# Packed attention into a two-product MoE layer: a first phase laid out as one written plan for five queues, with the first attention in parts of the array

## The chip, the cores and the metric

One core of a Trainium2 chip. The metric is the device time of one execution in microseconds (us), as a median of several runs. The profile is a separate execution, taken by the hardware profiler.

## The reference

Eight batches of eight heads, 576 rows of 64 numbers in each head. 32 packed queries `p` attend to `k` and `v`, the rows `q` attend to the result, and the outcome goes through two matrix products with a gate between them. The weights come as 64-bit floats, all else as 32-bit floats.

```python
def sm_attn(qq, kk, vv):                     # scale = 1/8
    s = scale * np.matmul(qq, kk.transpose(0, 1, 3, 2))
    a = np.exp(s - np.max(s, axis=-1, keepdims=True))
    a = a / (np.sum(a, axis=-1, keepdims=True) + 1e-09)
    return np.matmul(a, vv)
p_packed = sm_attn(p, k, v)                  # 8 x 8 x 32 x 64
x = sm_attn(q, p_packed, p_packed)           # 8 x 8 x 576 x 64, heads side by side: 4608 x 512
h = x @ w_in                                 # 512 x 2048
out = (h * np.clip(h + 3.0, 0.0, 6.0) / 6.0) @ w_out
```

## The kernel before

The kernel never forms `x`. For each batch it multiplies the packed result with `w_in` (this small product is called m) and then multiplies m with the attention weights of the rows (called a). Each 32-bit operand of a large product is split into a rounded part `hi` and a remainder `lo`, and three products (hi hi, hi lo, lo hi) are added in PSUM. w_in and w_out are cut into 16 pieces f of 128 columns or rows.

The work has two phases. The **first phase** computes the attention of the first batch, brings in the 32 pieces of the weights, narrows each to 32 bits, runs both large products of the first batch piece by piece as the weights arrive, and prepares the attention of the second batch. After it the weights are in SBUF, and seven batches follow in a **steady phase** (`moe`), in which each batch's products run beside the attention of the next.

Steps of the first phase and their names, with the lines of the profile:

- `first_attention` turns k, p and q with TensorE against an identity (L494 to L550), forms the first scores in two groups of four heads (`s1`, L565, L573), their exponentials on ScalarE (L588), the packed result (`pack`, L616, then `u_ppt0`), the second scores (`s2`, L636: eight products of 128 by 64 and a rest of 64 rows for each group), their softmax with rows as partitions (L660 to L680, the last product by GpSimd for group 0), and turns the result back with TensorE (L689) before the split into a_hi and a_lo (L695, L698). The code's order of calls is the order on each engine.
- `load_w` loads a piece (L122, 512 KB). A piece is narrowed in four steps (`narrowed`): two on ScalarE (L139, L141), a shift on VectorE (L145), an addition on GpSimd (L149). A piece of w_out is then split by ScalarE (L159) and VectorE (L161). Each of the two kinds has two load buffers, so that a load waits for the narrowing of the piece two before it; pieces 2 and 3 go to spare room.
- `u_m0` (L193, L204, L206) makes m for a piece, `gemm1` (L448, twelve matmuls) the first product into the one PSUM tile `ps_h`, L951 (ScalarE) and L952 (VectorE) the gate, L960 (ScalarE) and L962 (GpSimd) the split into gh and gl, L961 and L963 the same for the last 64 columns, and `gemm2` (L853, twelve matmuls) the second product one piece later.
- `attention(1)` runs in between: from f = 4 on, the loop over f takes three steps of it for each f, one ahead of the first product and two behind the second.

The order in this loop is that of the code, a whole piece f at a time. Five queues carry it: TensorE (PE), VectorE (DVE), ScalarE (ACT), GpSimd (POOL) and SyncE (SP), which issues the loads. For four of them the order is fixed by hand; the scheduler places SP's. TensorE's warm-up matmuls (L722, on zeros) stand at five places, 11 in all.

Of the kernel before, what the change touches and what calls it, by code (L numbers as in the profile page):

```python
# [20 lines left out]

FIRST_AHEAD = 4
PER_FIRST_STEP = (1, 2)
# [3 lines left out]
IN_ORDER = 4  # L27


WARM = (3, 2, 2, 1, 3)  # L30
# [3 lines left out]
def packed_attention_moe(  # L34
# [46 lines left out]
    wo_hi = const.tile([P, NF, DM], F32R, name="wo_hi")  # L81
    wo_lo = const.tile([P, NF, DM], F32R, name="wo_lo")
# [21 lines left out]

    wide_in = w_in.dtype == I64
# [3 lines left out]
    def load_w(f, names=("in", "out")):  # L109

        for name in names:
            src = (w_in_v if name == "in" else w_out_v)[f]
            if name == "in" and not wide_in:
                raw = w_in_at(f)
            elif f in (2, 3) and wide_in:
                if f not in early:
                    early[f] = wr.tile([P, 2, 2 * DM], I32, name=f"raw{f}", tag=f"w_in{f}")
# [7 lines left out]
    def narrowed(f, name):  # L125
# [24 lines left out]
        state["w", name, f] = x  # L150

# [3 lines left out]
    def w_out_step(f):  # L155
        yield from narrowed(f, "out")
        yield
        x = state.pop(("w", "out", f))
        nc.scalar.copy(out=wo_hi[:, f], in_=x)  # L159
        yield  # L160
        nc.vector.tensor_sub(out=wo_lo[:, f], in0=x, in1=wo_hi[:, f].bitcast(F32))  # L161

    raws, early = {}, {}

    def step(part, n=1):
        for _ in range(n):
            next(part, None)
# [5 lines left out]

    def att_ps():
        return ps_a.tile([P, 512], F32, name="ps1", tag="att")

    state = {}

# [8 lines left out]
    def u_m0(f, bank=att_ps):  # L187

        x = state.pop(("w", "in", f))
        ps = bank()  # L190
# [15 lines left out]
        nc.vector.tensor_sub(out=lo[:, :, fs], in0=psv, in1=hi[:, :, fs].bitcast(F32))  # L206

# [66 lines left out]
    def u_s1(b):  # L274
# [4 lines left out]
        for hf in range(2):  # L279
            for x, s in enumerate(scores(pt, kt, hf)):  # L280
                nc.scalar.copy(out=e[x][:, hf * HS:(hf + 1) * HS], in_=s)
                nc.vector.reduce_max(out=mx[x][:, hf:hf + 1], in_=s, axis=AX.X)
            yield
        for x in range(2):
# [3 lines left out]
            )  # L288
            den = sm.tile([P, 1], F32, name="den")
            nc.scalar.activation(  # L290
# [3 lines left out]
            rinv = sm.tile([P, 1], F32, name="rinv")  # L294
            nc.vector.tensor_scalar_add(den, den, 1e-9)
            nc.vector.reciprocal(rinv, den)
            state["e", b, x] = (e[x], rinv)

    def u_et(b, x):
# [3 lines left out]
        for c in range(4):  # L303
            nc.tensor.transpose(out=ps[:, c * P:(c + 1) * P], in_=e[:, c * P:(c + 1) * P], identity=ident)  # L304
        nc.scalar.copy(out=et[:, :4 * P], in_=ps)
        yield
        ps = att_ps()
        nc.tensor.transpose(out=ps[:REM, :P], in_=e[:, 4 * P:S], identity=ident)
        nc.vector.tensor_copy(out=et[:REM, 4 * P:], in_=ps[:REM, :P])
        state["et", b, x] = et  # L310

    def u_pv(b, x):
# [17 lines left out]
        nc.vector.tensor_scalar_mul(state["pn", b][:, x], ps[:, :D], rinv)  # L330

# [6 lines left out]

    def u_ppt0(g, bank):
        pn = state.pop(("pn", 0, g))  # L340
        ps = bank()
        nc.tensor.transpose(out=ps[:, :P], in_=pn, identity=ident)
        yield
        pv = ps[:, :P].rearrange("p (x n) -> p x n", x=2)
        for h in range(2):
            nc.vector.tensor_copy(
                out=pp_bd[64 * h:64 * h + 64, 2 * g:2 * g + 2, NPK * h:NPK * h + NPK],
                in_=pv[64 * h:64 * h + 64, :, NPK * h:NPK * h + NPK],
            )

    def u_s2(b):
        qt = [state.pop(("q", b, a)) for a in range(NPAIR)]
        z = [ap.tile([P, T, NPK], F32, name="z", tag="e", bufs=4) for _ in range(2)]
        for hf in range(2):
            for x, s in enumerate(scores(pps[b % 2], qt, hf)):
                nc.vector.transpose(out=z[x].rearrange("p t n -> p (t n)")[:, hf * HS:(hf + 1) * HS], in_=s)
            yield
# [3 lines left out]
    def u_a(b, x, z):  # L361

        mx = sm.tile([P, T], F32, name="mx2")
        nc.vector.reduce_max(out=mx, in_=z, axis=AX.X)
        nc.vector.tensor_sub(out=z, in0=z, in1=mx.unsqueeze(2).to_broadcast([P, T, NPK]))
        nc.scalar.activation(out=z, in_=z, func=AF.Exp, scale=scale)
        yield
        den = sm.tile([P, T], F32, name="den2")
        nc.vector.reduce_sum(out=den, in_=z, axis=AX.X)
        nc.vector.tensor_scalar_add(den, den, 1e-9)  # L370
        nc.vector.reciprocal(den, den)
        nc.vector.tensor_mul(out=z, in0=z, in1=den.unsqueeze(2).to_broadcast([P, T, NPK]))
        yield
        at = ap.tile([P, S], F32, name="at", tag="e", bufs=4)
        nc.vector.transpose(out=at, in_=z.rearrange("p t n -> p (t n)"))
        hi = ap.tile([P, S], F32R, name="a_hi", tag=f"a_hi{x}", bufs=2)
# [7 lines left out]
    def u_m(b, n):  # L384
        hi, lo = m_tiles(b, n)
        for x, ps in enumerate(each_head(pps[b % 2], lambda a, half: w_in_sb[n][half, :, a])):
            nc.scalar.copy(out=hi[:, x], in_=ps)  # L387
            nc.vector.tensor_sub(out=lo[:, x], in0=ps, in1=hi[:, x].bitcast(F32))  # L388

    def attention(b):  # L390


        def load(which, a):
            state["nat", which, b, a] = load_blocks(k if which == "k" else q, b, a)

        def turn(which, a):
            t = ap.tile([P, T, 32], F32, name="tr", tag="tr", bufs=4)
            nc.vector.transpose(out=t, in_=state.pop(("nat", which, b, a)))  # L398
            state[which, b, a] = t

        load_p(b)
        load("k", 0)
        load("k", 1)
        yield
        transpose_p(b)
        turn("k", 0)
# [632 lines left out]
```

## Time and profile before

| | |
|---|---|
| median of 3 runs | 759.91 us (758.5, 759.91, 763.88) |
| the profiled execution, its own time | 757.65 us |
| its span | 755.9 us |
| PE busy | 735.9 us, 97% of the span |
| DVE, ACT, POOL busy | 345.5, 387.2, 279.9 us (46%, 51%, 37%) |
| first product of the first batch starts (L448) | 30.61 us |
| first product of the second batch starts (L824) | 136.14 us |
| data moved | 55.98 MB, 26.6 MB of it in the first 140 us |

The trace is read by stretches: the first phase ends where the last L853 of the first batch ends, between 138 and 139 us. A matmul's end is modelled, and overlaps the next one's start, so the distance between starts tells the pace (0.133 us for 288 columns, 0.23 for 512). In a row of the timeline the first number is the start, the second the time; what stands in brackets is the idle time ahead of it, and what ended that.

### The profile page before, as it was taken

Reading aid. Unit: us, or ns where it says so; the run is one execution under the profiler, and the core shown is the slowest. Engines: PE = TensorE matmul, PEld = TensorE weight load, DVE = VectorE, ACT = ScalarE, POOL = GpSimd, SP = SyncE. Lnnn points to the kernel's source line nnn. Section 1 sums busy time; section 2 is a strip of 40 time slices with the busy share of each in tenths; the row PEclk is TensorE's granted clock in tenths of the full one; section 3 lists DMA queues with packets and bytes.
Section 4 is the critical chain, followed back from the end, with each engine's and each line's share of the span. In section 5 each row is a group of like instructions: output and inputs, shape, how many; then the busy total and the mean of one; then the engine's idle time right before and its main releaser. Section 6 shows DMA issues by size and latency. Waiting matters only on the chain.

```text
span 755.9 us, 13998 instructions
## 1 busy us (share of the span) xinstructions
PE 735.9 (97%) x5197; PEld 581.3 (77%) x5197; DVE 345.5 (46%) x714; ACT 387.2 (51%) x922; POOL 279.9 (37%) x415
## 2 busy tenths in 40 slices
PE   7898999999999999999999999999999999999998
PEld 5775776778777876878777886788787887788886
DVE  3676888432563365342733446342643527321121
ACT  4687874543445445553455535563354635553343
POOL 0487782422233224332333223333232333343332
PEclk9999899999999999999999999999999999999999
DMA  8869964104410541043310523024220210000010
GB/s 260 254 146 215 263 186 83 56 16 93 96 32 31 102 73 45 1 91 69 63 43 1 120 52 78 1 60 96 47 61 1 61 33 29 1 29 0 2 42 29
DMA packets 191205, 55.98 MB, mean 74 GB/s; under 512 B 173216, under 2 KB 184480, under 8 KB 191136
## 3 DMA queue, kind: packets, MB, share of 16 engines
q1 hardware_dynamic: 191136, 55.08, 31.5%
q8 instruction: 41, 0.67, 0.4%
q14 instruction: 28, 0.23, 0.1%
HBM read 45.61 MB, written 9.44 MB: 73 GB/s over the span
## 4 chain that ended last, share of the span: by engine, by line
PE 79%; DMA 6%; DVE 5%; SPq 4%; ACT 3%; issue 2%; POOL 1%; DVEq 0%; POOLq 0%; ACTq 0%
PE acc L853 46%; PE ps_hh L824 23%; PE ps L265 6%; SPq L213 3%; DMA raw_in<-in_moe_w_in_dram 2%; DMA nat<-in_q_dram 2%; PE ps L320 1%; DVE tr L398 1%; DMA nat<-in_k_dram 1%; PE ps_h L448 1%; PE ps L304 1%; DMA v_nat<-in_v_dram 1%; POOL x_out L149 1%; DVE w_in_sb L145 0%; ACT raw_in L139 0%
## 5 line engine op out<-in xcount | busy, mean ns | idle before, releaser
L842 POOL TENSOR_TENSOR g<-t,g 128x256 fp32r<-128x256 f32 x224 | 168.1, 754 | 410.0 <-ACT g L841 384.5
L853 PE MATMUL acc<-wo_hi,g 128*128 128x512 f32 x896 | 316.5, 394 | 1.3 <-ACT g L841 1.3
L837 DVE SCALAR_TENSOR_TENSOR t<-t,ps_hh 128x320 f32<-128x320 f32 (+1 forms) x224 | 100.1, 449 | 252.1 <-ACT t L836 252.0
L836 ACT ACTIVATE t<-ps_hh,three 128x320 f32<-128x320 f32 (+1 forms) x224 | 112.5, 503 | 177.9 <-PE ps_hh L824 167.1
L853 PEld LDWEIGHTS acc<-wo_hi,g 128*128 128x128 f32 x896 | 167.8, 188 | 35.8 <-issue 4.0
L853 PE MATMUL acc<-wo_lo,g 128*128 128x512 f32 x448 | 177.5, 396 | 0.0
L841 ACT CAST g<-t 128x256 fp32r<-128x256 f32 x224 | 90.4, 405 | 94.1 <-DVE t L837 92.8
L824 PE MATMUL ps_hh<-a_hi,m_hi 128*128 128x320 f32 (+1 forms) x448 | 136.1, 304 | 0.5 <-DVE t L837 0.5
L824 PE MATMUL ps_hh<-a_lo,m_hi 128*128 128x320 f32 (+1 forms) x448 | 132.7, 296 | 0.0
L824 PE MATMUL ps_hh<-a_hi,m_lo 128*128 128x320 f32 (+1 forms) x448 | 132.7, 296 | 0.0
L824 PEld LDWEIGHTS ps_hh<-a_hi,m_hi 128*128 128x128 f32 x448 | 84.4, 188 | 34.5 <-issue 19.5
L853 PEld LDWEIGHTS acc<-wo_lo,g 128*128 128x128 f32 x448 | 84.5, 189 | 11.9 <-issue 1.7
L824 PEld LDWEIGHTS ps_hh<-a_lo,m_hi 128*128 128x128 f32 x448 | 84.5, 189 | 8.2 <-issue 0.9
L824 PEld LDWEIGHTS ps_hh<-a_hi,m_lo 128*128 128x128 f32 x448 | 84.5, 189 | 1.7 <-issue 1.3
L398 DVE STREAM_TRANSPOSE tr<-nat 128x576 f32<-128x576 f32 x56 | 41.9, 765 | 30.9 <-PE ps L265 13.3
L388 DVE TENSOR_TENSOR m_lo<-ps,m_hi 128x512 fp32r<-128x512 f32 x56 | 36.1, 683 | 34.8 <-ACT m_hi L387 34.8
L848 POOL TENSOR_TENSOR bnd_lo<-t,bnd_hi 128x64 fp32r<-128x64 f32 x112 | 39.3, 351 | 0.0
L387 ACT CAST m_hi<-ps 128x512 fp32r<-128x512 f32 x56 | 30.1, 589 | 9.8 <-PE ps_hh L824 7.7
L265 PE MATMUL ps<-w_in_sb,pps 64*32 64x512 f32 x448 | 34.3, 601 | 0.5 <-DVE m_lo L388 0.5
L962 POOL TENSOR_TENSOR gl<-t,gh 128x512 fp32r<-128x512 f32 x16 | 23.4, 1464 | 20.6 <-ACT gh L960 11.8
L853 PE MATMUL acc<-wo_hi,gh 128*128 128x512 f32 x64 | 27.0, 421 | 3.5 <-ACT gh L960 3.5
L149 POOL TENSOR_TENSOR w_in_sb<-w_in_sb,raw_in 128x512 int32<-128x512 int32 x14 | 19.5, 1392 | 26.6 <-ACT raw_in L141 17.7
(170 smaller groups left out, 860.2 us busy)
## 6 DMA issues: line engine op xcount, KB each, us to landing
out_dram<-osb SPq DMA_DIRECT2D x36, 256.0 KB, 2.1
nat<-in_k_dram SPq DMA_DIRECT2D x112, 72.0 KB, 2.5
nat<-in_q_dram SPq DMA_DIRECT2D x112, 72.0 KB, 2.6
raw_in<-in_moe_w_in_dram SPq DMA_DIRECT2D x14, 512.0 KB, 5.9
raw_out<-in_moe_w_out_dram SPq DMA_DIRECT2D x14, 512.0 KB, 5.4
v_nat<-in_v_dram SPq DMA_DIRECT2D x56, 128.0 KB, 2.8
spare<-in_k_dram SPq DMA_DIRECT2D x2, 512.0 KB, 4.8
raw<-in_moe_w_in_dram SPq DMA_DIRECT2D x2, 512.0 KB, 4.1
```

Of the source, the lines that this page charges most:

```text
L149: nc.gpsimd.tensor_tensor(out=xi, in0=xi, in1=low, op=ALU.add)
L265: nc.tensor.matmul(banks[x][NPK * a:NPK * a + NPK, :n], rows[half, a], c, start=True, stop=True)
L387: nc.scalar.copy(out=hi[:, x], in_=ps)
L388: nc.vector.tensor_sub(out=lo[:, x], in0=ps, in1=hi[:, x].bitcast(F32))
L398: nc.vector.transpose(out=t, in_=state.pop(("nat", which, b, a)))
L824: nc.tensor.matmul(h[:, :n], mm[:, g, fs], aa[:, t0:t0 + n], start=(g == 0 and i == 0), stop=(g == NG - 1 and i == 2),)
L836: nc.scalar.activation(out=t[:, :n], in_=h, func=AF.Relu, bias=three)
L837: nc.vector.scalar_tensor_tensor(out=t[:, :n], in0=t[:, :n], scalar=6.0, in1=h, op0=ALU.min, op1=ALU.mult)
L841: nc.scalar.copy(out=gh, in_=tm)
L842: nc.gpsimd.tensor_sub(out=gl, in0=tm, in1=gh.bitcast(F32))
L848: nc.gpsimd.tensor_sub(out=bnd_lo[:, slot:slot + REM], in0=tb, in1=bh.bitcast(F32))
L853: nc.tensor.matmul(acc, gg, ww[:, f], start=(f == 0 and i == 0), stop=(f == NF - 1 and i == 2),)
```

## The change

Only the first phase's code changes; the seven later batches keep theirs, apart from the yields of its generators.

1. Every step becomes a chain, a generator that stops after each instruction. One written list of names (`PLAN`, some 500 entries) says which chain goes on next; SP's order is by hand now as well. The pieces f overlap freely in it.
2. A table (`ENGINES`) says which engine does certain copies and differences. All 16 differences gl move from POOL to DVE, ten of the 16 of the last 64 columns too; POOL keeps the additions and the difference of the first piece of w_out.
3. The first attention is rewritten. The second scores are formed like the first, by eight products of 32 by 256 and four of 64 by 32 in parts of the array (`products`); their softmax works on one 128x576 tile, turned by DVE instead of PE, and that of group 1 in two halves (`HALVES`). Copies into block form are POOL's. q is turned by transposes instead of products.
4. Its tiles live in the room that pieces 4 to 15 of w_out take later (`room`, given up at `below`). Two early loads are issued by ACT's queue.
5. Warm-up matmuls are 3 instead of 11.

```diff
+PLAN = """
+warm in in in in in li0 in k0 in li1 k1 k0 in p k1 in kr p in s0 p p kr s0 a0 lo0 a0 k3 in s0 lp warm s0 k3
...
+ENGINES = {
...
+    "gl3": "D", "bl3": "D", "wl5": "D", "gl4": "D", "bl4": "P", "wl6": "D", "gl5": "D", "bl5": "D",
...
+        def products(s, g, rows, cols, blocks, rest):
+            for h in range(4):
+                for x in range(2):
+                    half = slice(64 * x, 64 * x + 64)
+                    nc.tensor.matmul(s[32 * h:32 * h + 32, x, :2 * P], rows[half, 4 * g + h],
+                                     cols[2 * g + h // 2][half, h % 2], start=True, stop=True)
+            yield
...
+        def gates(f):
...
+            nc.scalar.activation(out=tv, in_=hv, func=AF.Relu, bias=three)
+            yield
+            nc.vector.scalar_tensor_tensor(out=tv, in0=tv, scalar=6.0, in1=hv, op0=ALU.min, op1=ALU.mult)
+            yield
...
+            nc.scalar.copy(out=hi, in_=top)
+            yield
+            on(f"gl{f}", "P").tensor_sub(out=lo, in0=top, in1=hi.bitcast(F32))
+            yield
...
-            nc.gpsimd.tensor_sub(out=gl, in0=t[:, :4 * P], in1=gh.bitcast(F32))
...
+    HAND.add(mybir.EngineType.SP)
...
+    with tc.manual_schedule(engines=HAND):
+        for name in PLAN.split():
...
+            elif name in chains:
+                next(chains[name])
```

In the plan `a` and `b` are the narrowing of a piece of w_in and w_out, `m`, `h`, `r`, `y`, `x` the steps of the products, `li` and `lo` the loads.

ACT at the start of the program, before: the exponentials of the first scores (L588, group 0 and then group 1) and the copies of the turned q, then the first weight to be narrowed (raw_in, L139).

```order
L500 COPY kt_155<-ps_t 128x512
L525 COPY p_bd<-ps_t 64x4x32 x2
L500 COPY kt_185<-ps_t 128x512
L588 ACTIVATE e_236,den_237<-ps_w,nb 128x512
L588 ACTIVATE e_236,den_237<-ps_w,nb 128x64
L541 COPY qt_226<-ps_t 128x512
L588 ACTIVATE e_241,den_242<-ps_w,nb 128x512
L588 ACTIVATE e_241,den_242<-ps_w,nb 128x64
L541 COPY qt_262<-ps_t 128x512
L139 ACTIVATE raw_in<-raw_in 128x512
```

The same place in the change (the exponentials are L664, the narrowing L180 and L182).

```order
L229 COPY room<-ps_t 128x512
L229 COPY room<-ps_t 128x256
L180 ACTIVATE raw_in<-raw_in 128x512
L182 ACTIVATE raw_in<-raw_in 128x512
L664 ACTIVATE e_195,den_196<-ps_w,nb 128x512
L229 COPY rows_209<-ps_t 128x512
L664 ACTIVATE e_195,den_196<-ps_w,nb 128x64
L180 ACTIVATE raw_in<-raw_in 128x512
L229 COPY room<-ps_t 64x128
```

The narrowing of piece 0 now stands ahead of the first exponential, and that of piece 1 ahead of the copy of its last 64 columns (64x128), which `pack` needs.

DVE in the loop over f, before, between two gates (L952): shifts (L145), differences of w_out (L161) and turns of the second batch's k (L398).

```order
L952 SCALAR_TENSOR_TENSOR t<-t,ps_h_808 128x576
L145 TENSOR_SCALAR x_out<-raw_out 128x512
L282 TENSOR_REDUCE mx<-ps_871 128x1
L282 TENSOR_REDUCE mx<-ps_872 128x1
L145 TENSOR_SCALAR x_out<-raw_out 128x512
L161 TENSOR_TENSOR wo_lo<-x_out,wo_hi 128x512
L952 SCALAR_TENSOR_TENSOR t<-t,ps_h_909 128x576
```

A stretch of the change of like place (the gate is L940, the shift L186, the difference of w_out L202, that of m L258).

```order
L940 SCALAR_TENSOR_TENSOR t<-t,ps_h_813 128x576
L342 TENSOR_SCALAR nb<-mx 128x1
L258 TENSOR_TENSOR m_lo<-ps_867,m_hi 128x2x128
L186 TENSOR_SCALAR x_out<-raw_out 128x512
L957 TENSOR_TENSOR bnd_lo<-t,bnd_hi 128x64
L947 TENSOR_TENSOR gl<-t,gh 128x512
L186 TENSOR_SCALAR w_in_sb_841<-raw_in 128x512
L940 SCALAR_TENSOR_TENSOR t<-t,ps_h_918 128x576
```

New between two gates are gl (L947), once for each f, and here the difference of the last columns (L957); both stood on POOL.

POOL in the loop, before: additions (L149) and, for each f, the two differences (L962, L963).

```order
L962 TENSOR_TENSOR gl<-t,gh 128x512
L963 TENSOR_TENSOR bnd_lo<-t,bnd_hi 128x64
L149 TENSOR_TENSOR w_in_sb_929<-w_in_sb_929,raw_in 128x512
L149 TENSOR_TENSOR x_out<-x_out,raw_out 128x512
L962 TENSOR_TENSOR gl<-t,gh 128x512
L963 TENSOR_TENSOR bnd_lo<-t,bnd_hi 128x64
L149 TENSOR_TENSOR x_out<-x_out,raw_out 128x512
```

In the change POOL is left with additions (L190) and a few of the short differences.

```order
L190 TENSOR_TENSOR x_out<-x_out,raw_out 128x512 x2
L190 TENSOR_TENSOR w_in_sb_841<-w_in_sb_841,raw_in 128x512 x2
L957 TENSOR_TENSOR bnd_lo<-t,bnd_hi 128x64
L190 TENSOR_TENSOR x_out<-x_out,raw_out 128x512
L190 TENSOR_TENSOR w_in_sb_841<-w_in_sb_841,raw_in 128x512
L957 TENSOR_TENSOR bnd_lo<-t,bnd_hi 128x64
```

An addition no longer waits behind a difference whose input comes from the gate. From the middle of the second batch on, the order on PE is the same in both kernels to the end.

More of the change, by code (lines that the diff above doesn't have):

```diff
@@ L172, in rest, with coarse @@
                 pass
+    def coarse(part):
+        for stop in part:
+            if stop is None:
+                yield
     def att_ps():
@@ L337, in u_ppt @@
         nc.vector.tensor_copy(out=pps[b % 2].rearrange("p a n -> p (a n)"), in_=ps[:, :P])
[L339 to L349, printed above, removed]
+        yield 1
     def u_s2(b):
@@ L384, in u_m @@
     def u_m(b, n):
+        banks = each_head(pps[b % 2], lambda a, half: w_in_sb[n][half, :, a])
+        yield
         hi, lo = m_tiles(b, n)
-        for x, ps in enumerate(each_head(pps[b % 2], lambda a, half: w_in_sb[n][half, :, a])):
+        for x, ps in enumerate(banks):
             nc.scalar.copy(out=hi[:, x], in_=ps)
+            yield
             nc.vector.tensor_sub(out=lo[:, x], in0=ps, in1=hi[:, x].bitcast(F32))
-    def attention(b):
[L393 to L399, printed above, removed]
+            yield
@@ L851, in second_product @@
     def second_product(f, acc, hi, lo):
-        for i, (gg, ww) in enumerate(((hi, wo_hi), (hi, wo_lo), (lo, wo_hi))):
+        for i, (gg, part) in enumerate(((hi, "hi"), (hi, "lo"), (lo, "hi"))):
             nc.tensor.matmul(
```

766 lines of the change are left out of this document (389 added, 377 removed), and 8 rows, old and new, of the table ENGINES.

## The prediction

> **What bounds the kernel now.** I read the page first, its shares and its slices, then the busy times by stretch.
>
> ```profile
> span 755.9 us, 13998 instructions
> PE 735.9 (97%) x5197; PEld 581.3 (77%) x5197; DVE 345.5 (46%) x714; ACT 387.2 (51%) x922; POOL 279.9 (37%) x415
> PE   7898999999999999999999999999999999999998
> ```
>
> The reader is to see that only the first eight or so slices (19 us each) have anything but PE in them: whatever is to be won lies in the first phase. The stretches show it in finer steps (columns: length, then busy time and instructions of PE, weight loads, DVE, ACT, POOL, then granted clock, DMA share, GB/s).
>
> ```profile
> 0.00:37.16 37.16, 30.90 (x300) 23.46 (x301) 19.96 (x55) 20.11 (x45) 9.03 (x20) 1.00 0.87 261
> 37.16:72.00 34.84, 33.94 (x215) 25.41 (x216) 23.94 (x36) 26.83 (x55) 28.25 (x26) 1.00 0.84 179
> 72.00:90.00 18.00, 13.27 (x104) 9.81 (x104) 15.01 (x28) 15.84 (x33) 12.01 (x10) 0.81 0.98 251
> 90.00:112.00 22.00, 21.77 (x180) 16.58 (x177) 18.38 (x27) 17.32 (x35) 18.60 (x16) 1.00 0.73 196
> 112.00:138.40 26.40, 24.48 (x160) 18.61 (x161) 20.48 (x33) 11.65 (x25) 9.97 (x10) 1.00 0.39 69
> 138.40:170.00 31.60, 31.60 (x207) 22.45 (x207) 11.27 (x23) 16.03 (x43) 8.91 (x19) 1.00 0.15 43
> ```
>
> From 138.4 us on PE is busy in all of the time, and DVE in a third of it. Since the order on PE is unchanged from the middle of the second batch on, a microsecond that the first phase ends earlier is one that the kernel ends earlier. The first phase has two parts with limits of their own, parted by the first matmul of piece 1 at 37.16.
>
> ```profile
> 37.16 0.40 PE L448 MATMUL ps_h<-a_hi,m_hi 128*128 128x288 f32 x1 [0.32 <-DVE t L952]
> 42.37 0.29 PE L448 MATMUL ps_h<-a_hi,m_hi 128*128 128x288 f32 x1
> 53.47 0.29 PE L448 MATMUL ps_h<-a_hi,m_hi 128*128 128x288 f32 x1
> 75.48 0.51 PE L853 MATMUL acc<-wo_hi,gh 128*128 128x512 f32 x1 [2.98 <-ACT gh L960]
> 137.75 1.09 PE L853 MATMUL acc<-wo_hi,gl 128*128 128x512 f32 x4
> ```
>
> Up to 37.16 a chain of dependent small steps sets the time; I call it the start. From there to 137.75 + 1.09 = 138.84, 101.7 us, runs the loop over the pieces. Where it is well fed, a piece takes PE 42.37 - 37.16 = 5.21 us. What PE needs for the second batch's attention shows in four rows.
>
> ```profile
> 70.66 0.72 PE L265 MATMUL ps<-tr,p_tr 64*32 64x288 f32 x16
> 83.08 0.60 PE L304 MATMUL ps<-ident,e 128*128 128x128 f32 x4
> 99.05 0.90 PE L320 MATMUL ps<-v_nat,et 128*32 128x64 f32 x40
> 128.85 1.08 PE L265 MATMUL ps<-w_in_sb,pps 64*32 64x512 f32 x14
> ```
>
> Four times 0.72, twice 0.60 and 0.3 for the fifth transpose, twice 0.90 and once 1.08 make 7.6. **PE's need in the loop** is thus 15 x 5.21 + 2.8 for the last second product + 7.6 = 88.6 us of the 101.7. Thirteen us are lost, in stalls like the 2.98 at 75.48 and in a lower clock after them (0.81 in 72 to 90).
>
> **The change, the start.** Its longest steps before:
>
> ```profile
> 8.95 0.66 PE L565 MATMUL ps_w<-kt,pt 64*32 64x256 f32 x16
> 11.09 0.69 ACT L588 ACTIVATE e<-ps_w,nb 128x512 f32<-128x512 f32 x1 [1.88 <-DVE nb L580]
> 16.39 1.10 PE L636 MATMUL ps_w<-pp_bd,qt 128*128 128x64 f32 x8 [0.26 <-DVE pp_bd L346]
> 18.35 0.33 PE L636 MATMUL ps_w<-pp_bd,qtr 128*64 128x64 f32 x2 [0.85 <-ACT qtr L557]
> 18.61 1.10 PE L636 MATMUL ps_w<-pp_bd,qt 128*128 128x64 f32 x8
> 27.44 0.66 PE L689 MATMUL ps_t<-ident,z 128*128 128x128 f32 x4
> 25.97 1.19 POOL L680 TENSOR_TENSOR z<-z,dn 128x256 f32<-128x256 f32 x2
> 11.07 0.60 SPq L122 DMA_DIRECT2D raw_in<-in_moe_w_in_dram  x1
> ```
>
> The second scores of group 0 now cost what the first do (0.66, and about 0.33 for the rest) instead of 1.10 + 0.33 + 1.10 and a second rest, 2.8: 1.8 us less, and 0.85 less where PE waited for the turned rest of q. The separate pieces of 64 rows go from four DVE steps (0.8 as an estimate, 0.2 each, what the steps of 0.33 on PE there take at the least). Against this stand two transposes out of PSUM and one in SBUF on DVE for the PE transposes (0.66 for four, and the hops), 0.5 more as an estimate, and POOL's copies into block form, which the rest of the scores waits for, 0.4 as an estimate (its two products of 256 columns took 1.19, the copies have 64 or 128). POOL keeps the product of group 0 (1.19 before, 1.3 for 576 columns). Together 2.5 less. Group 1 in halves and its earlier q give another 1.5 at piece 1.
>
> One edit costs. ACT now narrows piece 0 before the first exponential. The load of that piece is the fifth on SP's queue instead of the seventeenth, about 2.35 MB into the stream (k twice 0.52, v 0.59, the piece 0.52, p and the rest of k 0.2). In 0 to 37.16 us the DMA brought 261 GB/s, and 2.35 MB at that rate are 9.0 us after about 2 us without data: it lands at 11 or so. With two ACT steps ahead (0.68 each, L139's rows below) the exponential starts near 12.5, not 11.09: 1.5 us late. Sum of the start: -2.5 - 1.5 + 1.5 = **-2.5 us**. Bounds: +1.5 (the wait, and none of the rest shows) and -6 (no wait, hops shorter as well).
>
> **The change, the loop.** The 16 differences gl and ten of the short ones go from POOL to DVE; the pieces may overlap; loads, narrowing and the second batch's attention go between them by the plan. The work of DVE is the question. It was busy 23.94 + 15.01 + 18.38 + 20.48 = 77.8 us in the loop, POOL 68.8.
>
> ```profile
> L962 POOL TENSOR_TENSOR gl<-t,gh 128x512 fp32r<-128x512 f32 x16 | 23.4, 1464 | 20.6 <-ACT gh L960 11.8 <-ACT bnd_hi L961 8.8
> L161 DVE TENSOR_TENSOR wo_lo<-x_out,wo_hi 128x512 fp32r<-128x512 f32 x16 | 17.4, 1105 | 3.9 <-ACT wo_hi L159 3.8
> L963 POOL TENSOR_TENSOR bnd_lo<-t,bnd_hi 128x64 fp32r<-128x64 f32 x16 | 8.6, 540 | 0.0
> L145 DVE TENSOR_SCALAR x_out<-raw_out 128x512 int32<-128x512 int32 x14 | 11.3, 812 | 6.4 <-ACT raw_out L139 6.2
> 34.47 0.68 DVE L161 TENSOR_TENSOR wo_lo<-x_out,wo_hi 128x512 fp32r<-128x512 f32 x1
> L145 DVE TENSOR_SCALAR w_in_sb<-raw_in 128x512 int32<-128x512 int32 x14 | 8.9, 639 | 5.5 <-ACT raw_in L139 5.5
> 35.06 0.42 DVE L145 TENSOR_SCALAR x_out<-raw_out 128x512 int32<-128x512 int32 x1
> 38.70 1.51 DVE L145 TENSOR_SCALAR x_out<-raw 128x512 int32<-128x512 int32 x1
> 38.21 1.71 POOL L962 TENSOR_TENSOR gl<-t,gh 128x512 fp32r<-128x512 f32 x1
> ```
>
> A difference like gl takes DVE 0.68 us where POOL is idle, 1.1 on average; a shift 0.42 or, at 38.70, 1.51, and that one ended at 40.21, 0.3 after POOL's gl ended at 39.92. So these DVE steps wait for a POOL instruction under way. The average excess is 0.42 for a difference and about 0.31 for a shift (0.812 and 0.639 averaged, less 0.42), over 15 differences and 28 shifts in the loop 15 us. POOL loses 23.4 + 5.4 of its 68.8 us, so 0.58 of that excess should stay: 6.3 us less. gl then costs DVE 0.68 + 0.58 x 0.42 = 0.93, 16 of them 14.9; the ten short ones 2.5 at 0.25 each, an estimate between 0.14 (1.1 scaled to 64 columns) and POOL's 0.54; the one difference of w_out that goes to POOL gives 1.1 back. **DVE's need** is 77.8 + 14.9 + 2.5 - 1.1 - 6.3 = 87.8 us, as much as PE's 88.6. Bounds: 82 (no excess left) and 98 (1.1 for each and no relief).
>
> The DMA does not bind: up to 112 us its shares times lengths add to 95 us, by which time all weights had landed, and in the change the phase ends far later than that plus the last piece's ten us. ACT's work hardly changes; it was busy 71.6 of the loop's us.
>
> How full can PE be? In the pieces 1 to 4, ordered by hand without the second batch's attention, it reached 96% of its need's pace (16.3 us for three pieces, 37.16 to 53.47); over the rest 85%. The plan removes what cost most of the difference: an addition on POOL queued behind a gl that waits for the gate (20.6 us of POOL's idle time stood ahead of gl) held the load buffers, and whole pieces in a row held the steps of the next. With two engines needing 88 of the time I take 94%, 94.3 us instead of 101.7: **-7.4 us**. Bounds: 0 (85%, and DVE at its upper end) and -13.
>
> **The steady phase**: nothing, for and against, since PE is full there and keeps its order; moving the second batch's products of m by a few places costs nothing while DVE is busy in a third of the time.
>
> **Sum**: 757.65 (the profiled execution) - 2.5 - 7.4 = 747.8. The three runs lie 0.9 to 6.2 above the profiled execution; taking the 0.9 of the lowest, the forecast is **748.5 us**, the phase ending at about 129 in the profile.
>
> **Rivals.** *Deeper*: PE runs nearly at its need, 90 us for the loop, and the start brings 5. For it speaks that the plan orders single instructions on all queues; against it that three engines would have to be full at once. 757.65 - 5 - 11.7 + 0.9 = 742, from 736 to 744.
>
> *DVE becomes the bound*: gl behind POOL's additions costs 1.1 each, the relief does not come (98 us), and the gate waits in DVE's fixed order behind shifts whose loads are late. Then the loop gains 0 to 3 and the start 2.5: 753 to 757. For it speaks that every difference on DVE in the loop averaged 1.1; against it POOL's shorter work.
>
> *A cold clock in the start.* There are 3 warm-up matmuls instead of 11. What a pause costs shows after the stall at 72.
>
> ```profile
> 72.00:75.00 3.00, 0.50 (x3) 0.06 (x1) 2.76 (x4) 2.67 (x6) 1.32 (x2) 1.00 0.66 134
> 87.00:90.00 3.00, 3.00 (x51) 2.41 (x51) 3.00 (x4) 2.64 (x6) 3.00 (x3) 0.55 0.93 338
> 88.45 1.43 PE L320 MATMUL ps<-v_nat,et 128*32 128x64 f32 x40
> ```
>
> At a clock of 0.55 the same 40 matmuls took 1.43 us instead of 0.90. PE's steps on the start's chain (turns, both scores, the transposes of e, the packed product, the first product of piece 0) add to about 7 us; times 1.6 that is 4 more: 752.5. Against it: before, the clock stood at 1.00 throughout 0 to 37. The Trainium skill's page "TensorE: Matmul & The Clock Gate", in its part 1 on the HAM clock gate, says that TensorE starts at half clock and falls back to it after an idle window of about 3.4 us; by that rule the stall at 72 would cost what it did here, and a start with one early warm-up, before the first k lands, would run cold.
>
> *Slower*: ACT waits in its fixed order for a weight that lands later than the plan has it, with the gate of the next piece queued behind. ACT already stood idle for loads before:
>
> ```profile
> L139 ACT ACTIVATE raw_out<-raw_out 128x512 f32<-128x512 f32 x14 | 9.6, 684 | 5.9 <-DMA raw_out<-in_moe_w_out_dram 5.9
> L139 ACT ACTIVATE raw_in<-raw_in 128x512 f32<-128x512 f32 x14 | 9.6, 682 | 6.5 <-DMA raw_in<-in_moe_w_in_dram 6.4
> ```
>
> PE has about 3.4 us of other work (the 5.21 of a piece less its first product) to cover the gate's two steps, 1.5 together, so 1.9 of lateness is free. If twelve pieces are 3.4 us late, 12 x 1.5 = 18 us are lost: 766, and from a lateness of 2.8 on the change costs time. Against it: over half of the sixteen pieces would have to be that late.
>
> **How the numbers follow.** Chances: the forecast (744 to 752) 0.42, deeper 0.18, DVE the bound 0.20, cold start 0.08, slower 0.12. One per cent, 7.6 us, is about what a measurement can tell; it puts the bounds at 752.3 and 767.5. Faster by more: 0.42, 0.18 and a third of the cold start, some 0.63. Slower by more: half of the slower case, 0.06. Within: 0.31. The range runs from 737 to 761; below lies a third of the deeper case, above most of the slower one.
>
> **What would show it.** Piece 1's first matmul (L512) near 34.5 instead of 37.16; the first L664 near 12.5 behind a wait for raw_in; the last second product of the first batch near 129; gl on DVE at 0.9 on average, POOL's additions at 1.3 as before; DVE over 90% busy between; no stretch of 18 us with a clock of 0.8. Wrong would be the sum if PE's idle time in the loop is named after ACT behind raw tiles (slower), after gl with DVE full (the bound), or hardly at all (deeper).

## The result, and the profile after

The changed kernel takes **748.83 us** (median of 4 runs, 747.54 to 750.47) against 759.48 us (4 runs) of the kernel before in the same session: ratio 0.985, 95% interval 0.9806 to 0.9894, so 1.5% faster. The prediction said 748.5. The sum that led there has two wrong terms, whose errors cancel, and one misread row, though, and the experiments changed its reasons.

The page after, its span, shares and slices (19 us each):

```profile
span 745.8 us, 13906 instructions
PE 722.9 (97%) x5167; PEld 573.1 (77%) x5167; DVE 345.1 (46%) x736; ACT 385.7 (52%) x920; POOL 252.9 (34%) x392
PE   7699998999999999999999999999999999999998
```

The profiled execution took 747.54 us, 10.1 less than that of before. PE's busy time fell by 13.0 (735.9 to 722.9) and its idle time rose by 2.9 (20.0 to 22.9). In the start, where there are fewer warm-ups, it rose by 6.3 (6.26 to 12.56); in the loop it fell by 2.6. The stretches of the first phase after, with the columns of the prediction's table:

```profile
0.00:35.94 35.94, 23.38 (x279) 16.21 (x279) 21.80 (x54) 21.09 (x46) 12.47 (x23) 0.90 1.02 266
35.94:72.00 36.06, 34.28 (x231) 27.74 (x230) 26.91 (x51) 28.05 (x60) 17.25 (x16) 0.95 0.84 203
72.00:90.00 18.00, 16.58 (x141) 12.95 (x140) 12.95 (x25) 14.95 (x33) 10.41 (x10) 1.00 0.84 214
90.00:112.00 22.00, 22.00 (x196) 16.92 (x194) 18.56 (x41) 17.83 (x35) 10.65 (x9) 1.00 0.76 198
112.00:130.90 18.90, 16.95 (x104) 11.99 (x104) 16.88 (x34) 9.90 (x20) 1.39 (x2) 1.00 0.53 100
```

The row of the loop that differs most is 72 to 90: PE works 16.58 us of 18 at a clock of 1.00, where it worked 13.27 at 0.81 before. That is 3.3 us less idle time, and, as an estimate from the distances between the starts of matmuls, the halved clock cost 2.9 us there before. So the stalls of before at 72.5 to 75.48 and at 84, with the low clock behind each, are some 6 us of the loop's gain in this pair of profiled executions; the rest is in other places.

The loop's ends, and pieces 3, 4 and 7 on the way (single rows of PE's timeline, after; then piece 7 and the end before, whose other rows stand in the prediction):

```profile
35.94 0.61 PE L512 MATMUL ps_h<-a_hi,m_hi 128*128 128x288 f32 x1
48.17 0.40 PE L512 MATMUL ps_h<-a_hi,m_hi 128*128 128x288 f32 x1 [1.29 <-DVE t L940]
53.15 0.29 PE L512 MATMUL ps_h<-a_hi,m_hi 128*128 128x288 f32 x1
70.57 0.29 PE L512 MATMUL ps_h<-a_hi,m_hi 128*128 128x288 f32 x1
130.49 0.39 PE L872 MATMUL acc<-wo_hi,gl 128*128 128x512 f32 x1
```

```profile
81.38 0.40 PE L448 MATMUL ps_h<-a_hi,m_hi 128*128 128x288 f32 x1
142.56 0.39 PE L853 MATMUL acc<-wo_hi,gl 128*128 128x512 f32 x1
```

A second product is twelve matmuls; in the plan it goes on in four steps `x` of three. Piece 1 starts at 35.94 instead of 37.16, 1.2 us earlier. Piece 4 starts at 53.15 against 53.47, and two such steps of earlier pieces (1.4 us) are still to come, which before had done by then: by work done the changed kernel is 1 us behind. Piece 7 starts at 70.57 against 81.38, with six steps (4.1 us) still to come: 6.7 ahead. The gain of the start is used up by piece 4; most of what counts is made behind it, up to piece 9 (81.49 against 93.62, with three steps, 2.1 us, to come), where the lead is 10. In the profile of the repeat below, piece 4 is as far behind, and piece 7 (73.12) 4.1 ahead.

**A misread row.** The prediction took 137.75 + 1.09 = 138.84 for the end of the loop before. Those four matmuls belong to piece 14. The last second product of piece 15 ends at 142.56 + 0.39 = 142.95, as 130.49 + 0.39 = 130.88 does after. The loop of before was 105.8 us long, not 101.7, and the first phase did not end between 138 and 139 us, as the section on the profile before has it, either.

### The profile page after: what moved, and what is told of

It reads as the page before. It is cut to its first block, busy times and chain, and to the rows that moved or that the text cites. A ratio compares the mean times of both kernels' runs of the same rounds, so it can differ in the third digit from the quotient of the medians.

```text
span 745.8 us, 13906 instructions
## 1 busy us (share of the span) xinstructions
PE 722.9 (97%) x5167; PEld 573.1 (77%) x5167; DVE 345.1 (46%) x736; ACT 385.7 (52%) x920; POOL 252.9 (34%) x392
## 4 chain that ended last, share of the span: by engine, by line
PE 84%; DMA 5%; DVE 3%; ACT 3%; SPq 3%; issue 1%; POOL 1%; ACTq 0%; DVEq 0%; POOLq 0%
PE acc L872 49%; PE ps_hh L843 24%; PE ps L318 6%; SPq L266 2%; DMA raw_out<-in_moe_w_out_dram 2%; PE ps L382 1%; PE ps_h L512 1%; DMA nat<-in_k_dram 1%; DMA room<-in_k_dram 1%; PE ps L363 1%; DMA raw_in<-in_moe_w_in_dram 1%; DVE tr L459 1%; ACT t L938 0%; ACT raw_out L182 0%; POOL w_in_sb L190 0%
## 5 line engine op out<-in xcount | busy, mean ns | idle before, releaser
L843 PE MATMUL ps_hh<-a_hi,m_hi 128*128 128x320 f32 (+1 forms) x448 | 136.7, 305 | 0.0
L843 PE MATMUL ps_hh<-a_lo,m_hi 128*128 128x320 f32 (+1 forms) x448 | 133.0, 297 | 0.0
L843 PE MATMUL ps_hh<-a_hi,m_lo 128*128 128x320 f32 (+1 forms) x448 | 132.3, 295 | 0.0
L843 PEld LDWEIGHTS ps_hh<-a_hi,m_hi 128*128 128x128 f32 x448 | 84.2, 188 | 33.9 <-issue 20.8
L843 PEld LDWEIGHTS ps_hh<-a_lo,m_hi 128*128 128x128 f32 x448 | 84.6, 189 | 9.5 <-issue 1.8
L843 PEld LDWEIGHTS ps_hh<-a_hi,m_lo 128*128 128x128 f32 x448 | 84.6, 189 | 0.3
L512 PE MATMUL ps_h<-a_hi,m_hi 128*128 128x288 f32 x64 | 21.3, 333 | 7.4 <-ACT a_hi L780 4.5
L866 ACT CAST bnd_hi<-t 128x64 fp32r<-128x64 f32 x112 | 27.0, 241 | 0.0
```

What stands on the lines that cost most here:

```text
L512: nc.tensor.matmul(h[:, hf, :HS], mm[:, g, fs], aa[:, hf * HS:(hf + 1) * HS], start=(g == 0 and i == 0), stop=(g == NG - 1 and i == 2),)
L843: nc.tensor.matmul(h[:, :n], mm[:, g, fs], aa[:, t0:t0 + n], start=(g == 0 and i == 0), stop=(g == NG - 1 and i == 2),)
```

## The experiments

All ratios are against the kernel before on the same chip. In the text, "narrowing" is the four or five steps on a loaded weight, "gate" the three steps t, t, gh of a piece, and "the phase's end" the end of the last second product of the first batch.

**The change again.** No edit.

> The changed kernel once more, as the base for the others on this chip. Expected: 747 to 750 us, first matmul of piece 1 at 35.9, last second product of the first batch at 130.9 in the profile, and a clock of 0.5 between 30 and 39 us in this run too, since PE stands still for 4.5 us ahead of piece 0 in each run. If the low clock there was chance, it is at 1.0 here, and the time 2 to 3 us shorter.

749.17 us (748.95 to 750.45), 0.9868 [0.9839, 0.9897]. The clock on PE in the start differs between two runs of one program (first fence the first run, then this one; the seventh group of numbers is the clock):

```profile
30.00:33.00 3.00, 2.92 (x10) 2.74 (x11) 2.90 (x11) 2.68 (x6) 0.00 (x0) 0.50 1.36 222
33.00:36.00 3.00, 2.05 (x13) 1.38 (x12) 2.18 (x5) 2.02 (x4) 2.45 (x2) 0.50 1.25 223
36.00:39.00 3.00, 3.00 (x15) 3.00 (x14) 2.68 (x3) 1.69 (x5) 2.71 (x4) 0.50 1.03 358
```

```profile
30.00:33.00 3.00, 2.74 (x10) 2.56 (x11) 2.90 (x10) 2.67 (x7) 0.00 (x0) 0.50 1.31 252
33.00:36.00 3.00, 1.65 (x15) 1.24 (x15) 2.36 (x5) 2.18 (x5) 2.27 (x2) 0.99 1.29 184
```

The low clock comes with a wait of PE of 4.49 us ahead of the first product of piece 0, and lasts until 39 in one run and 33 in the other; the run with the shorter one is no faster, and by piece 3 the two are level (48.17 and 48.26). The Trainium skill's page "TensorE: Matmul & The Clock Gate", part 1 on the HAM clock gate, has the clock halve after an idle window of about 3.4 us and calls the number of slow matmuls variable from run to run, since the window runs free. The pause of 4.49 us and the two lengths agree with that. The length of a pause alone does not decide here, though: the clock also halved at pauses of 2.98 and 1.68 us (before, at 75.48 and 85.73), and stayed at 1.00 at one of 3.17 us (before_gate_first, below).

**No pause on PE** (keep_warm): sixteen idle matmuls in the pause.

```diff
+        def heat():
+            ps = tail()
+            for _ in range(16):
+                nc.tensor.matmul(ps[:, :2 * P], zeros[:, :P], zeros, start=True, stop=True)
+            yield
+        chains["heat"] = heat()
 ...
 PLAN
-... z0a m0 a2 m1 z1a z1a b0 ...
+... z0a m0 a2 m1 heat z1a z1a b0 ...
```

> 16 more warm-up matmuls fill PE's wait of 4.5 us ahead of the first product of piece 0. Theory (the pause lowers the clock, and the low clock is on the path): the twelve matmuls of pieces 0 and 1 go back from 0.24 to 0.133 us each, piece 1 starts 1.3 to 1.8 us earlier (34.2 to 34.6 instead of 35.94) and piece 2 2.5 to 3 us earlier; the kernel gains 2 to 3 us. Rival (the low clock is hidden by the waits for DVE, ACT and POOL there): the clock is 1.0 and the phase ends within 0.7 us of 130.9.

751.83 us (751.36 to 754.33), 0.9912 [0.9882, 0.9941]: slower than the repeat by 2.7. The clock was 1.00 from 27 to 36, but the filler was too long for the gap:

```profile
25.29 7.17 PE L803 MATMUL ps_t<-pps 128*128 128x256 f32 x32
```

Piece 0 began behind it, at 32.11, 3 us later than in the change (29.09). So the test does not price the low clock alone. What it does show: piece 1 began at 36.43, only 0.5 later, and the phase ended at 132.3, within the 130.9 to 132.7 of the two runs without it. The lost time appears behind the first phase, and half of it far later, at a place that the edit does not touch (last section).

**Narrowing piece 0 after the exponential** (late_narrow): entries of PLAN for the narrowing of pieces 0 and 1 (`a0`, `a1`, `b0`) moved back behind the first attention's exponentials, the fifth `z0a` forward, ahead of `li4`.

> ACT narrows piece 0 of w_in after the exponentials of group 0, and piece 0 of w_out after the exponential of the second scores, so that neither stands behind a load. Theory (each of the two waits is on the chain of the start): the first exponential at 10.9 to 11.0 instead of 12.07, the one of the second scores at 20.5 to 21 instead of 22.53, a_hi and piece 0 about 1.5 to 2 us earlier; piece 1 at 34.0 to 34.5, and 1 to 2 us off the kernel's time. Rival (loads and the clock set piece 1 anyway): the exponentials move, piece 1 stays within 0.5 of 35.94.

748.33 us (747.47 to 749.55), 0.9855 [0.9825, 0.9884]: the same as the change. The first exponential started at 11.10 instead of 12.07, but DVE then met the shift of w_out in front of its sums:

```profile
20.43 0.76 DVE L767 TENSOR_TENSOR z<-z,mx 128x576 f32<-128x576 f32 x1
23.98 0.43 DVE L187 TENSOR_SCALAR x_out<-raw_out 128x512 int32<-128x512 int32 x1 [2.79 <-ACT raw_out L181]
```

Piece 0 began at 30.26 instead of 29.09, piece 1 at 36.73 instead of 35.94, and the phase ended at 131.3. The wait moved from ACT to DVE, and nothing was won. With both edits together (late_warm):

> Both edits. If the two theories hold and add: piece 1 at 32.5 to 33, the phase ending 3 to 5 us earlier than 130.9, the kernel at 743.5 to 746. If the loop is bound by the loads of the weights, not by where it starts: the phase ends within 1 us of 130.9, whatever the start does.

750.93 us (750.41 to 751.85), 0.9889 [0.986, 0.9918]: piece 1 at 37.41, the phase's end at 131.4, within the 130.9 to 132.7 of the change. As in keep_warm, what is lost is lost behind the first phase.

**PE 7 us busier at piece 1** (pe_more): the same sixteen matmuls as entry `heat`, now directly ahead of `h1`.

> Sixteen idle matmuls of 256 columns stand on PE between the turn and the first products of piece 1; in an earlier run sixteen of them took 7.17 us. If PE sets the end of the loop after a later start (the prediction's sum passes the start on one to one), the last second product of the first batch moves from about 131 to about 137 to 138 and the time is some 6 to 7 us above the changed kernel, 755. If PE has slack in the loop, because it waits for the gate on DVE and ACT in any case (about 5 us of waits), no more than 1 to 4 us come through: 750 to 753.

754.35 us (753.81 to 756.93), 0.9928 [0.9903, 0.9954], 5.2 above the repeat of the change. Against the first run of the change, piece 1 starts at 42.44, 6.5 later; piece 4 (56.30) is 3.2 later, the phase's end (135.5) 4.7 later. About half of the delay comes through to piece 4, and more is lost further on (PE waits 2.07 ahead of piece 14, where the change waits 0.99). The first three pieces have 3 us of slack: there the change waits, 1.29 at 48.17 for one, for a gate on ACT behind a weight that was there only at 44.89, and runs in part at the halved clock. That is where the start's gain went.

**DVE 13 us busier** (gl_twice): the line of gl is written twice.

```diff
             on(f"gl{f}", "P").tensor_sub(out=lo, in0=top, in1=hi.bitcast(F32))
+            on(f"gl{f}", "P").tensor_sub(out=lo, in0=top, in1=hi.bitcast(F32))
```

> Each difference gl of the first phase is computed twice in place, which changes no value and adds sixteen instructions of 0.74 us, 11.8 us, to DVE. If DVE's need is what sets the loop, as the prediction had it (88 of 94 us), the time rises by 8 to 11 us, to 757 to 760. If DVE has the slack that its 75.3 busy us of 95 show, it rises by 0 to 4, to 749 to 753.

753.17 us (752.63 to 754.26), 0.9923 [0.9896, 0.9951]: 4.0 to 4.3 more. The loop in the change, and here:

```profile
35.94:130.90 94.96, 89.80 (x667) 69.60 (x666) 75.31 (x147) 70.73 (x145) 39.71 (x34) 0.98 0.76 183
```

```profile
36.10:135.02 98.92, 92.13 (x666) 68.84 (x665) 88.20 (x162) 71.71 (x145) 40.81 (x34) 0.99 0.73 176
```

DVE does 12.9 us more, and the time rises by a third of it. At 75.3 of 95 us DVE has slack, so it does not set the loop of the change. With DVE at 88.2, the need that the prediction gave it, the loop takes 98.9 us, not the 94.3 that the prediction took for two engines needing 88.

**The differences back on POOL** (gl_pool): in ENGINES every `gl` and `bl` becomes "P", the plan stays.

> The plan and everything else stay, but all gl and all short differences go back to POOL. If it is the plan that brings the loop's gain and the engine of gl matters little, the time stays within 1.5 us of the changed kernel, 748 to 751. If the gain came with the move of gl off POOL (DVE's other steps no longer wait for a POOL instruction under way, POOL's additions no longer stand behind gl), the differences of w_out on DVE go back to 1.0 us or so, POOL's idle time ahead of gl returns, and the time goes to 753 to 758.

748.03 us (747.2 to 748.82), 0.9846 [0.9807, 0.9885]: no difference to the change. The groups in the loop after, and here (columns: busy us, mean ns, idle ahead):

```profile
L947 DVE TENSOR_TENSOR gl<-t,gh 128x512 fp32r<-128x512 f32 x16 | 11.8, 738 | 3.3 <-ACT gh L945 3.3
L202 DVE TENSOR_TENSOR wo_lo<-x_out,wo_hi 128x512 fp32r<-128x512 f32 x15 | 11.2, 752 | 0.7 <-ACT wo_hi L200 0.6
```

```profile
L947 POOL TENSOR_TENSOR gl<-t,gh 128x512 fp32r<-128x512 f32 x16 | 22.2, 1391 | 15.8 <-ACT gh L945 8.3 <-DVE tr L459 4.2 <-PE ps_h L512 2.7
L202 DVE TENSOR_TENSOR wo_lo<-x_out,wo_hi 128x512 fp32r<-128x512 f32 x15 | 13.9, 935 | 1.1 <-ACT wo_hi L200 1.0
L186 DVE TENSOR_SCALAR x_out<-raw_out 128x512 int32<-128x512 int32 x12 | 8.6, 713 | 0.7 <-ACT raw_out L180 0.5
```

All that the prediction blamed is back: POOL stands 15.8 us idle ahead of gl with additions behind it, and DVE's other steps are longer. In this plan it costs nothing. The prediction was right about what the move of gl does to the durations, but the move has no part in the gain that shows.

**gl on DVE in the old order** (before_gl_dve): in the kernel before, the two differences of a piece move from `nc.gpsimd` to `nc.vector`, nothing else.

> The kernel before with gl and the short differences on DVE, and nothing else of the change. If the engine of gl is the larger part of the loop's gain, 753 to 756, with the differences of w_out on DVE near 0.75 us. If the plan is, DVE, whose order puts gl ahead of the next steps of narrowing, takes 15 us more for nothing: 759 to 764.

764.85 us (762.06 to 766.9), 1.0077 [1.0052, 1.0102]: slower by 0.8%. Alone, in the old order, the move loses. So it is not the engine of gl but the rest of the change, plan and start, that carries the gain; and of the start's gain nothing is left by piece 4.

**Gate first, in the kernel before** (before_gate_first). ACT in the kernel before ahead of the stall:

```profile
70.45 0.69 ACT L139 ACTIVATE raw_out<-raw_out 128x512 f32<-128x512 f32 x1 [1.58 <-DMA raw_out<-in_moe_w_out_dram]
71.03 0.67 ACT L141 ACTIVATE raw_out<-raw_out 128x512 int32<-128x512 uint32 x1
71.59 0.62 ACT L159 CAST wo_hi<-x_out 128x512 fp32r<-128x512 f32 x1
72.10 0.75 ACT L951 ACTIVATE t<-ps_h,three 128x576 f32<-128x576 f32 x1
73.18 0.67 ACT L139 ACTIVATE raw_in<-raw_in 128x512 f32<-128x512 f32 x1 [0.33 <-DMA raw_in<-in_moe_w_in_dram]
73.75 0.65 ACT L141 ACTIVATE raw_in<-raw_in 128x512 int32<-128x512 uint32 x1
74.30 0.61 ACT L159 CAST wo_hi<-x_out 128x512 fp32r<-128x512 f32 x1
74.81 0.62 ACT L960 CAST gh<-t 128x512 fp32r<-128x512 f32 x1
```

The gate's input was ready when PE ended the first product, at 68.9. It stood 3.2 us behind a weight that landed late and its narrowing, and its last step, gh, once more behind a narrowing. That is the stall at 75.48 of the prediction's first rows. My theory at this point: take the gate ahead there, and the loop's loss is gone.

```diff
-            rest(out_(f + 1))
-            step(out_(f + 2), 3 if f else 1)
+            with tc.issue_after(gate[0].ins):
+                rest(out_(f + 1))
+                step(out_(f + 2), 3 if f else 1)
```

> The kernel before with one constraint more: from piece 4 on, ACT may not take the narrowing of w_out ahead of the gate of the piece. In the trace of before the gate of one piece stood at 72.10 us behind a wait of 1.58 us for w_out and three steps of narrowing; PE stood idle from 72.5 to 75.48 and its clock fell to 0.68 after it. If that one place is where the loop of before lost most of what the change wins, the stall and the low clock of 72 to 90 go and the time falls by 4 to 7 us, to 752 to 755. If the loss only moves to another place (the weight that is narrowed later is then late for its products), it stays within 2 us of 759.

761.62 us (759.81 to 763.47), 1.0023 [0.9994, 1.0051]: nothing won. The wait at that place is gone (0.18 at 74.33), but in this profiled run the phase ended at 147.2, with the clock at 1.00 everywhere. So the low clock was not needed for the loss either. The kernel before itself says the same: in eleven of its executions on record the granted clock was 1.000 over the whole time, and they took 756.8 to 759.7 us, still some 9 us more than the change. PE now waits 3.17 us at 79.62, behind DVE, which waits for the second batch's q, and then for the gate at 86.88 (1.87) and 110.02 (2.51):

```profile
78.12 0.78 DVE L398 STREAM_TRANSPOSE tr<-nat 128x576 f32<-128x576 f32 x1 [3.21 <-DMA nat<-in_q_dram]
```

The theory of the one place fell; in this order the next late loads stall PE from other queues.

**Whole pieces on PE** (pe_blocks): in PLAN the four entries `x` of each piece move together behind the second `h` of the next piece, as in the kernel before.

> The changed kernel, but on PE the four second products of a piece stand in one block behind the first products of the next piece, as in the kernel before; the other engines keep their plan in the loop. If it is the overlap of the pieces on PE that brings the loop's gain, 752 to 756, with new waits of PE for the gate. If the order on ACT is what counts, within 1.5 us of the changed kernel, 748 to 751.

754.15 us (752.81 to 756.1), 0.9924 [0.9892, 0.9956]: 5.0 to 5.3 of the change's 10 to 11 us are gone again (4.6 against sp_free below, which ran on the same chip). The longest new wait, on DVE and then on PE, and the clock behind it:

```profile
112.23 0.31 DVE L295 STREAM_TRANSPOSE p_tr<-p_nat 128x128 f32<-128x128 f32 x1 [3.36 <-DMA p_nat<-in_p_dram]
114.07 0.78 DVE L460 STREAM_TRANSPOSE tr<-nat 128x576 f32<-128x576 f32 x1 [1.53 <-DMA nat<-in_k_dram]
114.78 0.44 DVE L411 STREAM_TRANSPOSE z<-ps 128x288 f32<-128x288 f32 x1
115.14 0.71 DVE L941 SCALAR_TENSOR_TENSOR t<-t,ps_h 128x576 f32<-128x576 f32 x1
```

```profile
116.00 0.58 PE L513 MATMUL ps_h<-a_hi,m_hi 128*128 128x288 f32 x1 [3.18 <-DVE t L941]
```

```profile
117.00:120.00 3.00, 3.00 (x18) 2.72 (x18) 3.00 (x7) 0.66 (x2) 0.35 (x1) 0.50 0.86 176
```

Once more a load at the head of a queue, here DVE's, with a gate (L941) behind it, and a pause of PE that halves its clock. This profiled run is the slowest of its kernel's five (756.1), so the one wait need not be in all of them. And the overlap is not what removed the stall of before at 72.5: without it there is none at that place either. From piece 4 to piece 10 this kernel takes 37.2 us (55.83 to 93.04), the kernel before 46.4 (53.47 to 99.88) for the same steps but 0.8 us of the second batch's, and the change 35.2, with 1.4 us of second products put off. The loss comes behind piece 10.

**The queue of loads left free** (sp_free): `HAND.add(mybir.EngineType.SP)` is removed.

> The changed kernel, but SP's queue is left to the scheduler, which moves some fifteen of its loads (v of the second batch ahead of a weight, one w_in ahead of a w_out). If the written order of the loads is a part of the gain, the waits of ACT for raw tiles grow and the time goes to 751 to 755; if the loads come as they come because buffers and the DMA set them, within 1.5 us, 748 to 751.

749.55 us (749.28 to 750.43), 0.9878 [0.9855, 0.99]: the same as the repeat. The written order of the loads is no part of the gain.

**Gates ahead, in the change** (gates_ahead), an attempt at a better kernel: in PLAN the first two `a5` go behind the third `r1`, the first `b5` behind the first `r2`, and the second `r13` and `r14` directly behind their first.

> The changed kernel with five entries of its plan moved, so that a gate's step no longer stands behind a wait for a load: on ACT the third step of the gate of piece 1 ahead of the narrowing of w_in of piece 5, and the first step of the gate of piece 2 ahead of that of w_out of piece 5; on DVE the second step of the gates of pieces 13 and 14 directly after their first. In the changed kernel PE waits 1.29 us for the gate at 48.17, 0.99 at 113.16 and 0.64 at 120.21. If a load wait ahead of a gate is what still costs time there, these waits shrink to under 0.3 each and the time falls by 2 to 3 us below the changed kernel, to 746. If the loads themselves are late, the waits come back at the weights (PE behind wo_lo or w_in_sb) and the time stays within 1.5 us, 747.5 to 750.5.

750.45 us (747.19 to 751.47), 0.988 [0.9849, 0.9912]: not better. The wait ahead of piece 3, at 48.17, is gone (it starts at 46.84), and the time is back two pieces later in a wait of 1.00 at 57.50 and at piece 14, where the load is now a turn that the scheduler put ahead of the gate:

```profile
113.26 0.78 DVE L460 STREAM_TRANSPOSE tr<-nat 128x576 f32<-128x576 f32 x1 [2.48 <-DMA nat<-in_k_dram]
113.97 0.72 DVE L941 SCALAR_TENSOR_TENSOR t<-t,ps_h 128x576 f32<-128x576 f32 x1
```

No version tried is faster than the changed kernel beyond the intervals.

## Why the prediction was right or wrong

**The start, -2.5: mis-sized**, -1.2 at piece 1. The first exponential came at 12.07 behind a wait for raw_in, as forecast (12.5); not in the sum were a second such wait of 2.02 us for raw_out at 20.25 and the low clock from 29 on. The 1.5 for group 1 was taken from no row. Its weight was wrong too: the sum passes the start on one to one, but by piece 4 nothing of it is left, and pe_more shows 3 us of slack there.

**The loop, -7.4: right in direction, base misread, size by a wrong reason.** With the ends corrected it went from 105.8 to 95.0, 10.8 less. Before, the loop held twelve first products of the second batch more (14 of L824 against 2 of L843, 1.8 us at 0.15 each), which the change does right after: 9.0 net. The 95.0 came close to the 94.3 forecast because the two numbers behind it nearly held: PE's need, 89.7 with the second group of 1.09 that the true end takes in, over 95.0 is a fill of 94%, what the prediction chose. That the sum gave 748.5 for 748.83 is luck all the same: the start was taken 1.3 too large, the loop 1.6 too small (-7.4 for -9.0), and the two errors cancel.

Of the 10.8 us, only 2.6 are idle time of PE (7.8 to 5.2); 8.2 are busy time. Besides the 1.8 put off, the halved clock stretched PE's work in the loop by some 2.9 us before and 1.2 after (an estimate, from the distances between starts). And the order within the second batch's attention counts: the same 96 products in parts of the array take PE 8.06 us before and 5.04 after (the two loops, before and then after; length, then busy time and count of PE and of its weight loads for these products alone):

```profile
37.16:142.95 105.79, 8.06 (x96) 1.60 (x96) 0.97 0.69 160
35.94:130.90 94.96, 5.04 (x96) 1.09 (x96) 0.98 0.76 183
```

Before, three of the six groups of sixteen are cut in two or three parts, and a part of two takes nearly as long as a whole group of sixteen does after:

```profile
58.42 0.67 PE L265 MATMUL ps<-tr,p_tr 64*32 64x288 f32 x2
64.16 0.69 PE L265 MATMUL ps<-tr,p_tr 64*32 64x288 f32 x10
66.40 0.68 PE L265 MATMUL ps<-tr,p_tr 64*32 64x288 f32 x4 [0.41 <-DVE tr L398]
```

```profile
55.52 0.72 PE L318 MATMUL ps<-tr,p_tr 64*32 64x288 f32 x16
```

The prediction's need of 7.6 for that attention counts whole groups, so it has this loss in the 13 us, under stalls.

**DVE's need, 87.8: wrong.** DVE was busy 75.3. gl took 0.74 instead of 0.93, and the excess of the differences of w_out nearly vanished (1.105 to 0.752) where I let 0.58 of it stay. The stated cause of the loop's loss, additions queued behind gl, is refuted by gl_pool, where they stand there again and the time stays; before_gl_dve agrees, though there DVE's queue gets longer as well. What the runs show in its place: loads come late in both kernels, and PE loses less by it in the change. By the waits, after and then before:

```profile
ACT raw_in L180 <- DMA raw_in<-in_moe_w_in_dram: 6.4, 6, 1.7
ACT raw_out L180 <- DMA raw_out<-in_moe_w_out_dram: 3.8, 5, 1.8
```

```profile
ACT raw_out L139 <- DMA raw_out<-in_moe_w_out_dram: 4.7, 4, 1.6
ACT raw_in L139 <- DMA raw_in<-in_moe_w_in_dram: 3.8, 6, 1.6
```

ACT waited 10.2 us for weights after (13.6 in the repeat) and 8.5 before, yet PE's idle time in the loop fell from 7.8 (105.79 less 98.02 busy) to 5.2. pe_blocks, with the overlap of pieces on PE taken out, returns half of the gain, in its profile behind piece 10. The other half, with the end of the stall at 72.5, is not pinned to one entry of the plan, and its cause stays open: the engine of gl, the order of loads and the order of the start's narrowing are excluded; whole groups in the second batch's attention are a part that the rows show and no run tests alone; of the rest, the order on ACT and DVE was only tried in single places.

**The steady phase, 0: right.** The gain is 12.1 us at the phase's end (142.95 to 130.88), 1.8 of it work put off, and 10.1 at the end of the kernel.

**The rivals.** *Deeper* did not come (95.0, not 90). *DVE the bound*: no, gl_twice. *Cold start*: the low clock came, at a place after the chain of exponentials that I had priced, in two runs for 3 and 10 us, without a price that shows; no run separates it from the pause. Up to 27 us the clock stood at 1.00, though there was one early warm-up. *Slower*: its mechanism, a gate behind a late weight on ACT, is at work in both kernels (the 2.98 at 75.48 before, the 1.29 at 48.17 after); I reckoned with it in the change alone.

**The signs.** The first exponential, POOL's additions (1.35 to 1.40) and the clock in the loop came as said; piece 1 (35.94 for 34.5), the end (130.88 for 129), gl (0.74 for 0.9) and DVE's share (79%, not over 90%) did not.

## What to carry to other kernels

In this kernel a wait for a load cost what stood behind it in its engine's queue, less the other work that the bounding engine had at hand: giving PE that work (second products split between the first products of the next pieces) won 5 us, while moving single waits out of the way won nothing in three attempts. Find the end of a phase by the last instruction of its tile, counted, and not by the last row in sight. A gain ahead of a stage that waits for loads is not passed on: check the slack of the next stage before adding it to the sum. Count the bounding engine's busy time as well as its idle time: most of this loop's gain was busy time.

## What was not expected of the hardware

The halved clock came in pieces of one length: by the clock's record in the traces, each stretch of it in the first phase is a multiple of 3.41 us, one (before, twice; the repeat), two (pe_blocks) or three (the change, 28.96 to 39.20).

SP's time to issue one DMA is not constant. In keep_warm eight loads of k take 0.3 to 0.5 us each to issue, except the sixth:

```profile
446.03 1.84 SPq L267 DMA_DIRECT2D nat<-in_k_dram  x1
```

DVE then waits for that k (`DMA nat<-in_k_dram`), a gate stands behind it, and PE loses 1.2 us at 453 and 457. In before the sixth load at the same place took 1.93, in late_warm 1.93, in pe_more 1.88, and PE waits there too (0.3, 1.2 and 1.1); in the two runs of the change the long issue (1.19 and 1.73) fell on a q that PE did not wait for. The orders of keep_warm on all queues are those of the change but for the filler. From the phase's end to the end of the program keep_warm takes 617.3 us, both runs of the change 614.9; 1.2 of these 2.4 come from where this long issue falls. What makes it long is open, and so is the rest.

That stretch took 613.8 to 617.3 us in the profiles of the changed kernel's variants, though none of their edits is aimed at it. A difference of two or three us between two variants is thus no measure of the first phase; the 4 and 5 us of gl_twice, pe_more and pe_blocks also show at the phase's end (135.0, 135.5 and 138.5, against 130.9 and 132.7).
